# A pre-norm linear-attention and FFN block on one core: one more transpose by DMA, two more FFN blocks in halves, and a new order table

## The chip, the cores and the metric

The kernel runs on one core of a Trainium2 chip. The metric is the device time of one execution in microseconds. Before the change three timed executions took 169.82 (the median), 169.5 and 170.22 us. One further execution was profiled; it took 169.75 us by the same clock, and the span of its trace, from the first to the last instruction, is 168.0 us.

## The reference, cut to what matters

The input x has 2048 tokens of 512 elements; there are 32 heads of 16 elements, and the FFN is 1792 wide. All tensors are bf16.

```python
def _A_ref(x, wqkv, wo):                 # linear attention
    q, k, v = split(x @ wqkv)            # H = 32 heads of Dh = 16
    phi = lambda t: jnp.where(t > 0, t + 1, jnp.exp(t)) + 1e-6
    pq, pk = phi(q), phi(k)
    kv  = jnp.einsum("bhsd,bhse->bhde", pk, v)
    z   = jnp.einsum("bhsd->bhd", pk)
    num = jnp.einsum("bhqd,bhde->bhqe", pq, kv)
    den = jnp.einsum("bhqd,bhd->bhq", pq, z)[..., None] + 1e-6
    return concat_heads(num / den) @ wo
def _B_ref(x, w1, w2):                   # FFN
    return jnp.maximum(x @ w1, 0) @ w2
h  = x + _A_ref(_layernorm(x), wqkv, wo)
h2 = h + _B_ref(_layernorm(h), w1, w2)
```

## The kernel before

**Tiles and stages.** The 2048 tokens are 16 tiles of 128 (t = 0 to 15) in four chunks of 512 (c = 0 to 3). The first stage normalizes the tiles, transposes each (tokens move from partitions to columns, `lnT0` to `lnT3`, one for each chunk), and multiplies by the key and query weights. The keys go through phi and are multiplied with the normalized input into the four PSUM banks 4 to 7, which serve as one accumulator over all tiles; a sum over the keys gives z. The second stage turns the accumulator into `kv` and then into one matrix `m_sb` for each group of heads, divides the queries by the denominator (which goes through DRAM to be spread over the partitions, tile `rr`), and forms h. The third stage normalizes h, transposes it into the same `lnT` tiles, and runs the FFN: `w1` blocks of 128 columns (f = 0 to 13) for each chunk, and then for each tile two runs of seven products with `w2`.

**What sets the order.** Nothing is scheduled by a planner. The text `ORDER` lists every step, in the order in which it is written; each engine takes its own steps in the order of the list and waits by semaphores for what they need. A word is a step and its numbers:

- `lx`, `lk`, `lq`, `lv`, `lo`, `l1`, `l2`: loads of x and the weights, all on SP's DMA queue.
- `S`, `A`, `R`, `N` (`s`, `a`, `r`, `n`, `nA` for the second norm): statistics (VectorE, DVE for short), aggregate (DVE), 1/std (ScalarE, ACT), normalized tile (DVE; `nA` on ACT).
- `T.t.bank` with `E.t`: transpose of tile t on TensorE (PE), four products of 128 x 128 into a bank, and its copy to `lnT` on ACT. `X.t` (and `x.t` for the second norm): the same transpose by one DMA on SP's queue, without PE, PSUM and ACT.
- `K.t.bank`: four products of a tile with the key weights. `F`, `U` (ACT: exp, relu), `M`, `D` (DVE: min, sum) make phi of two tiles. `Q.c.j.bank` with `qF`, `qU`, `qM`, `qD`: the same for the queries.
- `G.t`: four products of tile t into the accumulator. `za`, `zf`, `zhi`, `zlo` (DVE), `z` (PE), `zc`, `zh` (DVE): the sum over the keys. `gA`, `gD`, `kv`, `kx`, `m`, `mA`, `mD`: from the accumulator to `m_sb`.
- `d4`, `dl4`, `dx4`, `wb`, `rb`, `ab`, `dm`: denominator, its reciprocal, its way through DRAM (`wb` writes, eight `rb` or `ab` read into `rr`), and the product with the queries. `h.t.bank` and `hD.t`: h of a tile, and its sum with x.
- `p.c.f.bank`: block f of chunk c for all 512 tokens, four products of 512 columns. `ph.c.f.bank.half`: the same for 256 tokens, four products of 256 columns into half of a bank. `pD` (DVE), `pA` (ACT): relu of two neighbouring blocks. `f.t.bank.f0.n`: n of the fourteen products of tile t with `w2`. `fo` (DVE), `fd` (SP): the output and its DMA.

The numbers also choose the PSUM bank, so a step waits for the last reader of its bank. PE takes about 900 products in the order of the list, and what stands behind a waiting product waits too. SP's queue holds the loads, the DMA transposes, the way of the denominator and the outputs, one behind the other.

The lines that the steps below rest on:

```python
op_X = lambda t: nc.sync.dma_start_transpose(out=lnT_of(t), in_=ln_nat[:, t, :])     # L314
op_x = lambda t: nc.sync.dma_start_transpose(out=lnT_of(t), in_=hn[:, t % NQ, :])    # L315
def op_ph(c, f, b, half):
    cols = slice(half * CW // 2, (half + 1) * CW // 2)
    for kd in range(KD):
        nc.tensor.matmul(bk[:, b, cols], lhsT=w1_sb[:, kd, f * P : (f + 1) * P],      # L526
                         rhs=lnT[c][:, kd, cols], ...)
for word in ORDER.split():
    name, *idx = word.split(".")
    ops[name](*map(int, idx))
```

Line numbers of the profile: L293 `T`, L303 `E`, L314 `X`, L322 `K`, L330 `Q`, L340/L343 `F`/`U` and their query forms, L347/L350 `M`/`D`, L374 `G`, L398 `z`, L477 `rb`, L493 `dm`, L502 `h`, L517 `p`, L526 `ph`, L537 `pD`, L546 `f`, L554 `fo`.

Of the kernel before, what the change touches and what calls it, by code (L numbers as in the profile page):

```python
# [16 lines left out]

ORDER = """
table const lx.0.1 warm.66.7.64 lx.1.1 masks lx.2.1 lk.0.4 lx.3.1 S.0 lx.4.2 S.1 lx.6.2 lq.0.4 A.0 A.1 S.2 R.0.1
warm.2.7 lx.8.4 R.1.1 N.0 lx.12.4 A.2 N.1 T.0.1 R.2.1 T.1.5 E.0 N.2 E.1 T.2.2 S.3 K.0.0 E.2 A.3 S.4 K.2.2.2.2  # L20
R.3.1 K.2.2.0.2 F.0.1 N.3 S.5 U.0.1 T.3.3 K.1.6.0.2 E.3 A.4 A.5 K.1.6.2.2 S.7 R.4.2 K.3.1.0.2 M.0.1 F.1.1 S.6
K.3.1.2.2 U.1.1 Q.0.1.5 N.4 F.2.1 A.6 N.5 A.7 F.3.1 T.4.6 M.1.1 X.5 D.0.1 Q.0.0.4 R.6.2 D.1.1 M.2.1 U.3.1 M.3.1
Q.0.2.0 N.7 lo.0.2 E.4 S.9 X.7 U.2.1 Q.0.3.1 N.6 qU.0.0.2 D.3.1 K.4.2 S.15 X.6 qF.0.0.2 S.8 K.5.3 D.2.1 qM.0.0.2
qF.0.2.2 G.3 A.8 A.9 S.12 R.8.2 G.0 S.14 F.4.2 N.9 G.2 A.12 N.8 X.9 U.4.2 S.13 G.1 A.15 A.14 A.13 qD.0.0.2 X.8
R.12.2 K.6.2 qU.0.2.2 M.4.2 S.11 K.7.3 lv.0.2 R.14.2 N.12 N.13 X.12 K.9.1 S.10 F.6.2 D.4.2 K.8.0 U.6.2 lv.2.2 A.10
M.6.2 X.13 G.4 N.14 U.8.2 N.15 D.6.2 G.5 X.15 F.8.2 za.4.1 G.6 A.11 X.14 M.8.2 K.12.0 R.10.2 qM.0.2.2 N.10 K.13.1
N.11 X.10 D.8.2 G.7 za.6.0 F.12.2 X.11 K.14.2 U.12.2 qD.0.2.2 K.15.3 M.12.2 l1.2.2 za.8.0 l2.0.7 K.10.0 F.14.2
D.12.2 K.11.1 U.14.2 zf G.9 M.14.2 F.10.2 D.14.2 G.8 U.10.2 zhi M.10.2 G.12 zlo D.10.2 G.14 z.1.0 z.2.0 z.3.0
z.0.0 G.15 zc zh d4.0.3 G.11 dl4.0 dx4.0 G.10 wb.0 G.13 lo.2.2 Q.1.0.1 gA.2.2 gD.0.2 rb.0.6 Q.1.1.2 ab.0.3 rb.0.2
ab.0.7 rb.0.4 kv.0.0 kv.2.0 ab.0.1 rb.0.0 kv.1.0 kv.3.0 ab.0.5 l1.0.2 Q.1.3.6 kx qF.1.0.2 Q.1.2.5 qU.1.0.2  # L30
qM.1.0.2 m.0.3 m.1.4 Q.2.3.7 qF.1.2.2 mD.0.2 Q.2.1.1 qU.1.2.2 qM.1.2.2 dm.0.0.2 m.2.3 m.3.4 Q.2.0.0 dm.0.2.2
mA.2.2 qD.1.0.2 h.1.6 qU.2.0.2 qD.1.2.2 h.0.2 hD.1 qF.2.0.2 h.3.3 s.1 hD.0 Q.2.2.6 a.1 s.0 nA.1 d4.1.2 a.0 h.2.1
hD.3 x.1 nA.0 s.3 qF.2.2.2 Q.3.0.5 x.0 a.3 hD.2 dl4.1 Q.3.3.4 n.3 qU.2.2.2 s.2 x.3 Q.3.2.3 a.2 dx4.1 n.2 Q.3.1.6
qM.2.0.2 qF.3.2.2 x.2 qM.2.2.2 ph.0.2.0.0 qU.3.2.2 qM.3.2.2 ph.0.3.1.0 wb.1 ph.0.0.2.0 qF.3.0.2 qD.3.2.2
ph.0.1.3.0 qD.2.2.2 ph.0.1.3.1 qU.3.0.2 ph.0.0.2.1 qM.3.0.2 rb.1.6 p.0.11.7 rb.1.3 pD.0.0.2 rb.1.1 ph.0.3.1.1
rb.1.0 p.0.10.6 qD.2.0.2 rb.1.7 qD.3.0.2 rb.1.4 p.0.9.2 rb.1.2 pD.0.10.2 rb.1.5 p.0.6.5 l2.7.7 d4.2.6.2 ph.0.2.0.1
dl4.2 p.0.5.4 r.0.4 dm.1.0.2 dl4.3 p.0.4.3 dx4.2 dm.1.2.2 h.4.7 pD.0.2.2 wb.2 pA.0.4.2 p.0.7.6 dx4.3 hD.4 p.0.8.1
pD.0.6.2 h.5.7 pD.0.8.2 rb.2.4 p.0.13.4 rb.2.7 rb.2.3 hD.5 h.6.5 rb.2.0 rb.2.6 f.1.2.0.7 hD.6 rb.2.5 s.5 rb.2.2
rb.2.1 p.0.12.3 wb.3 h.7.1 pD.0.12.2 f.0.7.7.7 hD.7 s.4 f.2.4.0.7 s.7 a.5 a.4 dm.2.0.2 f.1.2.7.7 n.4 dm.2.2.2 a.7
n.5 rb.3.2 s.6 rb.3.6 h.9.0 rb.3.3 h.8.1 x.4 hD.9 a.6 f.0.7.0.7 n.7 r.4.4 fo.1 x.7 n.6 s.9 f.3.5.0.7 rb.3.1 x.6  # L40
h.10.0 x.5 h.11.3 f.3.5.7.7 f.2.4.7.7 fo.3 hD.8 fd.3 rb.3.7 p.1.13.2 fo.2 rb.3.4 fd.1 hD.11 p.1.12.1 rb.3.5 a.9
fo.0 fd.2 p.1.2.6 rb.3.0 hD.10 p.1.3.7 pD.1.12.2 p.1.6.0 pD.1.2.2 p.1.0.3 dm.3.0.2 p.1.7.1 dm.3.2.2 h.13.7
pD.1.6.2 p.1.1.4 hD.13 p.1.4.5 pD.1.0.2 p.1.5.6 s.13 p.1.9.3 pD.1.4.2 h.12.7 p.1.8.2 hD.12 s.10 p.1.11.5 s.8
p.1.10.4 pD.1.8.2 h.14.1 s.11 h.15.7 hD.14 a.10 f.7.0.0.7 a.11 n.9 hD.15 n.11 pD.1.10.2 f.6.7.0.7 a.8 n.10 r.8.4
s.14 x.10 f.4.1.0.7 n.8 x.8 f.5.5.0.7 x.9 f.5.5.7.7 x.11 f.4.1.7.7 fo.5 fd.0 s.12 a.13 f.7.0.7.7 a.12 fo.4 a.14
f.6.7.7.7 fo.7 n.14 n.12 s.15 p.2.10.5 fo.6 p.2.11.6 n.13 fd.6 a.15 n.15 r.12.4 x.12 p.2.13.1 p.2.12.0 fd.5 x.13
p.2.9.4 pD.2.12.2 p.2.8.3 x.15 p.2.2.1 pD.2.8.2 x.14 p.2.3.2 pD.2.10.2 p.2.0.3 fd.7 pD.2.2.2 p.2.1.4 p.2.7.6
pD.2.0.2 p.2.6.5 p.3.8.1 pD.2.6.2 p.3.9.2 p.3.12.3 pD.3.8.2 p.3.13.4 p.3.2.0 pD.3.12.2 p.2.4.6 p.3.10.5 p.3.6.1
p.2.5.7 p.3.4.3 pD.2.4.2 p.3.5.4 p.3.7.2 f.11.7.0.7 pD.3.6.2 pD.3.4.2 f.11.7.7.7 p.3.3.1 f.10.3.7.7 pD.3.2.2
p.3.11.6 p.3.0.4 pD.3.10.2 f.8.1.0.7 f.10.3.0.7 p.3.1.5 f.8.1.7.7 pD.3.0.2 fo.10 f.15.0.0.14.3.1 f.15.6.0.14.0.2  # L50
fo.15.3.1 fd.15.3.1 f.13.4.0.7 fo.15.0.2 fd.15.0.2 fd.4 f.13.4.7.7 f.14.5.7.7 fo.13 fo.11 fd.13 fd.10 f.12.6.0.7
fo.8 fd.8 fd.11 f.14.5.0.7 f.9.7.0.7 f.9.7.7.7 f.12.6.7.7 fo.9 fo.14 fd.9 f.15.3.0.14.2.1 fd.14 fo.12 fd.12
fo.15.2.1 fd.15.2.1
"""

# [541 lines left out]
```

## Time and profile before

| quantity | value |
|---|---|
| timed executions | 169.5, 169.82 (median), 170.22 us |
| profiled execution | 169.75 us, span of its trace 168.0 us |
| PE busy | 161.2 us, 96% of the span |
| DVE busy | 114.3 us, 68% |
| ACT busy | 49.4 us, 29% |
| TensorE clock granted | 0.999 |
| DMA | 16.28 MB in 26091 packets |

A few matmul records are missing from the trace (896 matmuls beside 912 weight loads), so a single short hole between two products can be a missing record. PE is shown busy until the modelled end of a product; the products themselves follow each other at 0.216 us for 512 columns.

### The profile page before, as it was taken

The page shows a single profiled execution, that of the slowest core. Times are in us where ns is not written, and L with a number is a line of the kernel's source. Part 1 is how long each engine was busy: PE and PEld are TensorE (multiplying, and loading weights), DVE is VectorE, ACT ScalarE, POOL GpSimd, SP SyncE. Part 2 cuts the span into 40 slices and gives each one's busy share as a digit, 9 for nine tenths or more (in the row PEclk, how much of TensorE's full clock was granted, in tenths as well). Part 3 has the DMA queues.
Part 4 walks back from the last instruction along what each step waited for, and adds up shares of the span by engine and source line. Part 5 has one row for each costly group of instructions (what it writes and reads, how often), then busy time and mean ns, then how long its engine had stood idle before and what let it go on. Part 6 is the DMA issues. An engine that isn't in the chain of part 4 may idle for free.

```text
span 168.0 us, 2376 instructions
## 1 busy us (share of the span) xinstructions
PE 161.2 (96%) x896; PEld 78.3 (47%) x912; DVE 114.3 (68%) x215; ACT 49.4 (29%) x83; POOL 4.8 (3%) x21
## 2 busy tenths in 40 slices
...
GB/s 112 328 313 156 58 182 105 234 238 96 205 138 35 119 92 248 98 105 7 109 71 153 5 4 0 31 102 23 125 94 4 0 0 0 0 0 59 125 0 101
DMA packets 26091, 16.28 MB, mean 97 GB/s; under 512 B 16096, under 2 KB 25056, under 8 KB 26080
## 3 DMA queue, kind: packets, MB, share of 16 engines
...
q8 instruction: 7, 0.11, 0.3%
q14 instruction: 4, 0.03, 0.1%
HBM read 9.96 MB, written 2.62 MB: 75 GB/s over the span
## 4 chain that ended last, share of the span: by engine, by line
PE 84%; DVE 6%; DMA 4%; issue 1%; ACT 1%; SPq 1%; DVEq 0%
PE bk L546 29%; PE bk L517 27%; PE bk L374 8%; PE bk L322 7%; PE bk L502 6%; PE bk L330 4%; DMA x_nat<-in_A_x_dram 2%; DVE h_nat L508 2%; DMA lnT<-hn 1%; PE bk L526 1%; DVE st L256 1%; DVE st L254 1%; SPq L220 1%; DVE pqT L350 1%; PE bk L398 1%
## 5 line engine op out<-in xcount | busy, mean ns | idle before, releaser
L546 PE MATMUL bk<-w_sb,at 128*128 128x512 bf16 (+2 forms) x245 | 49.4, 355 | 0.4
L517 PE MATMUL bk<-lnT,w_sb 128*128 128x512 bf16 x205 | 46.7, 379 | 0.1
L537 DVE TENSOR_SCALAR at<-bk 128x1024 bf16<-128x1024 f32 x27 | 32.5, 1219 | 16.2 <-PE bk L517 15.0
L546 PEld LDWEIGHTS <-at 128*128 128x128 bf16 x252 | 23.5, 98 | 25.2 <-DVE at L537 0.3
L517 PEld LDWEIGHTS <-w_sb 128*128 128x128 bf16 x208 | 20.4, 98 | 23.9
L554 DVE SCALAR_TENSOR_TENSOR gT<-bk,rstd,h_nat 128x512 bf16<-128x512 f32 (+2 forms) x18 | 12.1, 685 | 19.3 <-PE bk L546 13.9
L260 ACT ACTIVATE rstd<-mv,eps 128x2 f32<-128x2 f32 (+2 forms) x14 | 4.1, 293 | 51.7 <-DVE mv L257 48.9
L340 ACT ACTIVATE eb<-bk 128x1024 bf16<-128x1024 f32 (+1 forms) x18 | 16.6, 931 | 4.4 <-PE bk L322 2.6
L343 ACT ACTIVATE rb<-bk 128x1024 bf16<-128x1024 f32 (+1 forms) x18 | 16.5, 930 | 0.0
L502 PE MATMUL bk<-m_sb,pqs 128*128 128x512 bf16 x64 | 15.6, 379 | 0.0
L330 PE MATMUL bk<-lnT,wq_sb 128*128 128x512 bf16 x61 | 15.0, 379 | 0.2
L322 PE MATMUL bk<-wk_sb,lnT 128*128 128x512 bf16 x64 | 14.8, 379 | 0.0
L374 PE MATMUL bk<-at,h_nat 128*128 128x512 bf16 x54 | 13.0, 379 | 0.1
L508 DVE TENSOR_TENSOR h_nat<-bk,x_nat 128x512 bf16<-128x512 f32 x16 | 10.9, 681 | 1.7 <-PE bk L502 1.7
L254 DVE BATCH_NORM_STATS2 st<-x_nat 128x6 f32<-128x512 bf16 x16 | 10.6, 677 | 2.0 <-DMA x_nat<-in_A_x_dram 2.0
L256 DVE BATCH_NORM_STATS2 st<-h_nat 128x6 f32<-128x512 bf16 x16 | 10.8, 685 | 0.1
L502 PEld LDWEIGHTS <-pqs 128*128 128x128 bf16 x64 | 6.2, 98 | 7.6 <-DVE pqs L493 0.5
L374 PEld LDWEIGHTS <-h_nat 128*128 128x128 bf16 x64 | 6.1, 98 | 7.3 <-issue 0.2
L330 PEld LDWEIGHTS <-wq_sb 128*128 128x128 bf16 x64 | 6.2, 98 | 7.1
L322 PEld LDWEIGHTS <-lnT 128*128 128x128 bf16 x64 | 5.9, 98 | 7.5 <-DMA lnT<-h_nat 0.7
L347 DVE TENSOR_SCALAR eb<-eb 128x1024 bf16<-128x1024 bf16 (+1 forms) x18 | 6.7, 386 | 0.7 <-ACT eb L340 0.7
L493 DVE TENSOR_TENSOR pqs<-pqT,rr 128x1024 bf16<-128x1024 bf16 x8 | 5.2, 680 | 1.9 <-DMA rr<-scr 1.9
...
## 6 DMA issues: line engine op xcount, KB each, us to landing
w_sb<-in_B_w_dram SPq DMA_DIRECT2D x4, 896.0 KB, 5.0
...
```

Of the source, the lines that this page charges most:

```text
L254: op_S = lambda t: nc.vector.bn_stats(out=st[:, t, :], in_=x_nat[:, t, :])
L256: op_s = lambda t: nc.vector.bn_stats(out=st2[:, t, :], in_=h_nat[:, t, :])
L322: nc.tensor.matmul(bk[:, b, :], lhsT=lnT[c][:, kd, j * P : (j + 1) * P], rhs=wk_sb[:, kd, :], **part(("k", t), KD),)
L330: nc.tensor.matmul(bk[:, b, :], lhsT=wq_sb[:, kd, j * P : (j + 1) * P], rhs=lnT[c][:, kd, :], start=(kd == 0), stop=(kd == KD - 1),)
L340: nc.scalar.activation(out=buf(eb, kind, i, n), in_=bank(at_bank[kind, i], n), func=ACT.Exp)
L343: nc.scalar.activation(out=buf(rb, kind, i, n), in_=bank(at_bank[kind, i], n), func=ACT.Relu)
L374: nc.tensor.matmul(bk[:, KD + kd, :], lhsT=ln_nat[:, t, kd * P : (kd + 1) * P], rhs=pk(t)[:, 0, :], start=(not stated), stop=(len(stated) ...
L502: nc.tensor.matmul(bk[:, b, :], lhsT=pqs[:, (c * KD + jb) % NQ, j * P : (j + 1) * P], rhs=m_sb[:, jb, :], start=(jb == 0), stop=(jb == KD ...
L508: nc.vector.tensor_tensor(out=h_nat[:, t : t + n, :], in0=bank(at_bank["h", t], n), in1=x_nat[:, t : t + n, :], op=ALU.add,)
L517: nc.tensor.matmul(bk[:, b, :], lhsT=w1_sb[:, kd, f * P : (f + 1) * P], rhs=lnT[c][:, kd, :], start=(kd == 0), stop=(kd == KD - 1),)
L537: nc.vector.tensor_scalar(out=acts[c % 2][:, f : f + n, :], in0=bank(at_bank["p", c, f], n), scalar1=-1.0, scalar2=0.0, op0=ALU.mult, op1= ...
L546: nc.tensor.matmul(bk[:, b, 0 : w * P], lhsT=acts[c % 2][:, f, j * P : (j + 1) * P], rhs=w2_sb[:, f, k * P : (k + w) * P], **part(("f", t, ...
```

## The change

Only the text `ORDER` is changed; no step's code is.

- Tile 4 of the first norm: `T.4.6` and `E.4` are gone, `X.4` is there instead.
- The first chunk's FFN blocks 10 and 11 are now written in halves, as 0 to 3 were: six blocks of half 0 stand ahead of the first block of half 1, where it was four.
- The order of nearly all other steps and the banks of most are new.

A few lines of the diff; all that is changed reads like this:

```diff
-K.3.1.2.2 U.1.1 Q.0.1.5 N.4 F.2.1 A.6 N.5 A.7 F.3.1 T.4.6 M.1.1 X.5 D.0.1 Q.0.0.4 R.6.2 D.1.1 M.2.1 U.3.1 M.3.1
+N.5 Q.0.3.1 M.0.1 X.5 F.1.1 A.7 A.6 D.0.1 R.6.2 Q.0.0.6 N.4 M.1.1 U.3.1 N.6 X.4 Q.0.1.7 N.7 U.2.1 D.1.1 F.2.1 S.8
...
-qM.2.0.2 qF.3.2.2 x.2 qM.2.2.2 ph.0.2.0.0 qU.3.2.2 qM.3.2.2 ph.0.3.1.0 wb.1 ph.0.0.2.0 qF.3.0.2 qD.3.2.2
-ph.0.1.3.0 qD.2.2.2 ph.0.1.3.1 qU.3.0.2 ph.0.0.2.1 qM.3.0.2 rb.1.6 p.0.11.7 rb.1.3 pD.0.0.2 rb.1.1 ph.0.3.1.1
+n.2 qD.2.0.2 x.2 ph.0.2.6.0 qF.3.2.2 qM.2.2.2 ph.0.0.2.0 qD.2.2.2 ph.0.3.7.0 qF.3.0.2 rb.1.5 qM.3.2.2 ph.0.1.3.0
+rb.1.3 ph.0.11.1.0 qU.3.0.2 rb.1.1 qM.3.0.2 ph.0.10.0.0 qD.3.2.2 rb.1.6 ph.0.10.0.1 rb.1.7 qD.3.0.2 ph.0.3.7.1
```

**SP's queue, first norm.** The rows from the last loads of x to the first load of an FFN weight, before; `lnT1` to `lnT3` take the tiles of chunks 1 to 3, and one row can stand for several DMAs (x2, x3).

```order
L220 DMA x_nat_70<-in_A_x_dram 128x2048 x2
L314 DMA_TRANSPOSE lnT1_86<-h_nat_84 128x4x128
L226 DMA wo_sb_74<-in_A_wo_dram 128x2x512
L314 DMA_TRANSPOSE lnT1_86<-h_nat_84 128x4x128 x2
L314 DMA_TRANSPOSE lnT2_87<-h_nat_84 128x4x128 x2
L226 DMA wv_sb_73<-in_A_wqkv_dram 128x2x512
L314 DMA_TRANSPOSE lnT3_88<-h_nat_84 128x4x128
L226 DMA wv_sb_73<-in_A_wqkv_dram 128x2x512
L314 DMA_TRANSPOSE lnT3_88<-h_nat_84 128x4x128 x3
L314 DMA_TRANSPOSE lnT2_87<-h_nat_84 128x4x128 x2
L226 DMA w1_sb_75<-in_B_w1_dram 128x2x1792
```

The same place now:

```order
L220 DMA x_nat_70<-in_A_x_dram 128x2048 x2
L314 DMA_TRANSPOSE lnT1_86<-h_nat_84 128x4x128 x4
L226 DMA wv_sb_73<-in_A_wqkv_dram 128x2x512 x2
L314 DMA_TRANSPOSE lnT2_87<-h_nat_84 128x4x128 x2
L314 DMA_TRANSPOSE lnT3_88<-h_nat_84 128x4x128 x4
L314 DMA_TRANSPOSE lnT2_87<-h_nat_84 128x4x128 x2
L226 DMA w1_sb_75<-in_B_w1_dram 128x2x1792
```

Chunk 1 has four DMA transposes instead of three, the load of `wo` is out of their way, and both loads of the value weights stand ahead of the eight transposes of chunks 2 and 3, which are now unbroken.

**SP's queue, second norm of chunk 0.** From the way of the first denominators (`scr0`, `rr`) to that of the third (`scr2`), before and then now; the four transposes into `lnT0` are `x.1`, `x.0`, `x.3`, `x.2` in both.

```order
L477 DMA rr_113<-scr0_114 16x4x512 x4
L226 DMA w1_sb_75<-in_B_w1_dram 128x2x1792
L315 DMA_TRANSPOSE lnT0_85<-hn_119 128x4x128 x4
L474 DMA scr1_115<-rd_112 128x512
L477 DMA rr_113<-scr1_115 16x4x512 x8
L226 DMA w2_sb_76<-in_B_w2_dram 128x7x512
L474 DMA scr2_116<-rd_112 128x512
L477 DMA rr_113<-scr2_116 16x4x512 x8
```

```order
L477 DMA rr_113<-scr0_114 16x4x512 x4
L226 DMA w2_sb_76<-in_B_w2_dram 128x7x512
L315 DMA_TRANSPOSE lnT0_85<-hn_119 128x4x128 x2
L474 DMA scr1_115<-rd_112 128x512
L315 DMA_TRANSPOSE lnT0_85<-hn_119 128x4x128 x2
L477 DMA rr_113<-scr1_115 16x4x512 x8
L474 DMA scr2_116<-rd_112 128x512
L226 DMA w2_sb_76<-in_B_w2_dram 128x7x512
L474 DMA scr3_117<-rd_112 128x512
L477 DMA rr_113<-scr2_116 16x4x512 x8
```

The write of the second denominators (`wb.1`, into `scr1`) has moved between the second and the third transpose; the first half of `w2` (`l2.0.7`), which was loaded in the first stage, is now loaded between `wb.2` and `wb.3`, ahead of the eight reads of `scr2`.

**DVE, second norm of chunk 0.** From `hD.3` (sum with x of tile 3) on, before and then now; L276 is the normalized tile that a DMA transpose waits for, `n.3` first, `n.2` second.

```order
L508 TENSOR_TENSOR h_nat_84<-bk_120,x_nat_70 128x512
L256 BN_STATS st2_106<-h_nat_84 128x6
L257 BN_AGGR mv2_107<-st2_106 128x2
L508 TENSOR_TENSOR h_nat_84<-bk_120,x_nat_70 128x512
L276 TENSOR_SCALAR hn_119<-h_nat_84,mv2_107 128x512
L256 BN_STATS st2_106<-h_nat_84 128x6
L257 BN_AGGR mv2_107<-st2_106 128x2
L276 TENSOR_SCALAR hn_119<-h_nat_84,mv2_107 128x512
```

```order
L508 TENSOR_TENSOR h_nat_84<-bk_120,x_nat_70 128x512
L256 BN_STATS st2_106<-h_nat_84 128x6
L508 TENSOR_TENSOR h_nat_84<-bk_120,x_nat_70 128x512
L257 BN_AGGR mv2_107<-st2_106 128x2
L347 TENSOR_SCALAR eb_109<-eb_109 128x1024
L276 TENSOR_SCALAR hn_119<-h_nat_84,mv2_107 128x512
L256 BN_STATS st2_106<-h_nat_84 128x6
L257 BN_AGGR mv2_107<-st2_106 128x2
L276 TENSOR_SCALAR hn_119<-h_nat_84,mv2_107 128x512
```

One min of the queries (L347, `qM.2.0`) has moved ahead of `n.3`.

More of the change, by code (lines that the diff above doesn't have):

```diff
@@ L19 @@
 table const lx.0.1 warm.66.7.64 lx.1.1 masks lx.2.1 lk.0.4 lx.3.1 S.0 lx.4.2 S.1 lx.6.2 lq.0.4 A.0 A.1 S.2 R.0.1
-warm.2.7 lx.8.4 R.1.1 N.0 lx.12.4 A.2 N.1 T.0.1 R.2.1 T.1.5 E.0 N.2 E.1 T.2.2 S.3 K.0.0 E.2 A.3 S.4 K.2.2.2.2
-R.3.1 K.2.2.0.2 F.0.1 N.3 S.5 U.0.1 T.3.3 K.1.6.0.2 E.3 A.4 A.5 K.1.6.2.2 S.7 R.4.2 K.3.1.0.2 M.0.1 F.1.1 S.6
-K.3.1.2.2 U.1.1 Q.0.1.5 N.4 F.2.1 A.6 N.5 A.7 F.3.1 T.4.6 M.1.1 X.5 D.0.1 Q.0.0.4 R.6.2 D.1.1 M.2.1 U.3.1 M.3.1
-Q.0.2.0 N.7 lo.0.2 E.4 S.9 X.7 U.2.1 Q.0.3.1 N.6 qU.0.0.2 D.3.1 K.4.2 S.15 X.6 qF.0.0.2 S.8 K.5.3 D.2.1 qM.0.0.2
@@ L24 @@
[L24 to L33, printed above, removed]
@@ L34 @@
-qM.2.0.2 qF.3.2.2 x.2 qM.2.2.2 ph.0.2.0.0 qU.3.2.2 qM.3.2.2 ph.0.3.1.0 wb.1 ph.0.0.2.0 qF.3.0.2 qD.3.2.2
-ph.0.1.3.0 qD.2.2.2 ph.0.1.3.1 qU.3.0.2 ph.0.0.2.1 qM.3.0.2 rb.1.6 p.0.11.7 rb.1.3 pD.0.0.2 rb.1.1 ph.0.3.1.1
-rb.1.0 p.0.10.6 qD.2.0.2 rb.1.7 qD.3.0.2 rb.1.4 p.0.9.2 rb.1.2 pD.0.10.2 rb.1.5 p.0.6.5 l2.7.7 d4.2.6.2 ph.0.2.0.1
-dl4.2 p.0.5.4 r.0.4 dm.1.0.2 dl4.3 p.0.4.3 dx4.2 dm.1.2.2 h.4.7 pD.0.2.2 wb.2 pA.0.4.2 p.0.7.6 dx4.3 hD.4 p.0.8.1
-pD.0.6.2 h.5.7 pD.0.8.2 rb.2.4 p.0.13.4 rb.2.7 rb.2.3 hD.5 h.6.5 rb.2.0 rb.2.6 f.1.2.0.7 hD.6 rb.2.5 s.5 rb.2.2
@@ L39 @@
[L39 to L52, printed above, removed]
+warm.2.7 lx.8.4 R.1.1 lx.12.4 A.2 N.0 R.2.1 N.1 T.0.6 N.2 T.1.4 E.0 T.2.1 E.1 K.0.6 S.3 A.3 S.5 K.1.7.0.2 R.3.1
```

29 lines of the change are left out of this document (added).

## The prediction, made before the changed kernel was run

> **What bounds the kernel now.** First the page: busy shares and the shares of the chain that ended last.
>
> ```profile
> span 168.0 us, 2376 instructions
> PE 161.2 (96%) x896; PEld 78.3 (47%) x912; DVE 114.3 (68%) x215; ACT 49.4 (29%) x83; POOL 4.8 (3%) x21
> PE 84%; DVE 6%; DMA 4%; issue 1%; ACT 1%; SPq 1%; DVEq 0%
> ```
>
> PE is the bound, and both reorderings can only win what PE loses in waits. So the second view is the busy time by stage, with the cuts set where the chain leaves PE (columns: window, then PE, PEld, DVE, ACT, POOL busy with counts, clock, DMA share, GB/s).
>
> ```profile
> 6.70:36.30 29.60, 29.42 (x178) 13.72 (x179) 27.87 (x69) 23.79 (x42) 0.00 (x0) 1.00 0.69 199
> 36.30:56.10 19.80, 19.62 (x106) 8.98 (x108) 13.67 (x27) 13.90 (x17) 0.00 (x0) 1.00 0.39 108
> 56.10:58.70 2.60, 2.00 (x18) 1.63 (x18) 1.75 (x5) 2.60 (x4) 0.00 (x0) 1.00 0.58 124
> 58.70:165.00 106.30, 105.52 (x522) 49.99 (x531) 67.17 (x102) 5.71 (x14) 0.00 (x0) 1.00 0.21 59
> ```
>
> From 6.7 us on PE is full but for the third window: 0.60 us idle in 2.6. What remains in the fourth row is mostly missing records and the end of PE's work before 165. The third view, PE's timeline and the chain there, says what the hole is (start, duration, then the group).
>
> ```profile
> 56.09 1.92 PE L526 MATMUL bk<-lnT,w_sb 128*128 128x256 bf16 x16
> 58.62 1.03 PE L526 MATMUL bk<-lnT,w_sb 128*128 128x256 bf16 x8 [0.60 <-DMA lnT<-hn]
> ...
> 56.14 2.43 DMA lnT<-hn
> 59.65 0.86 PE bk L517 x4
> 60.51 0.44 PE bk L526 x4
> ```
>
> The sixteen products of the four half-0 blocks start at 56.09. A block in halves costs 0.44 for four products, 0.109 each, against 0.86 in full, so they are through at 56.09 + 16 x 0.109 = 57.84. The next product, of half 1, needs `x.2`, issued at 56.14 and landed 2.43 later, at 58.57. It starts at 58.62: **0.78 us lost**, of which the profile calls 0.60 idle because it lets the last product end 0.17 after its issue slot.
>
> **The change part by part.** The sum is made against the profiled execution, 169.75 us, which lies 0.07 under the median, 169.82.
>
> *Six blocks in halves.* Work: two more blocks cost 2 x (2 x 0.44 - 0.86) = 0.04 at most. Cover: six half-0 blocks fill 6 x 0.44 = 2.62 us, two blocks or 0.87 more than now. The hole goes if `x.2` lands no more than 0.1 later relative to PE. The rows behind `x.2`:
>
> ```profile
> 49.63 0.69 DVE L256 BATCH_NORM_STATS2 st<-h_nat 128x6 f32<-128x512 bf16 x1
> 50.83 0.17 DVE L257 BATCH_NORM_AGGREGATE mv<-st 128x2 f32<-128x6 f32 x1
> 51.78 5.57 SPq L315 DMA_TRANSPOSE lnT<-hn  x4
> 57.45 0.53 SPq L474 DMA_DIRECT2D scr<-rd  x1
> 51.04 1.58 ACT L282 ACTIVATE hn<-h_nat,mv 128x512 bf16<-128x512 bf16 x2 [1.00 <-DVE mv L257]
> 53.90 0.35 DVE L276 TENSOR_SCALAR hn<-h_nat,mv 128x512 bf16<-128x512 bf16 x1
> 55.09 0.35 DVE L276 TENSOR_SCALAR hn<-h_nat,mv 128x512 bf16<-128x512 bf16 x1
> ```
>
> Now SP's queue binds itself: `n.3` is done at 54.25 and `n.2` at 55.44, and SP comes to `x.2` at 56.14, 4.36 after `x.1`, and to `x.3` one transpose (1.3) earlier. In the new order `a.1` no longer stands behind `hD.0`: it can start when `s.1` ends, at 50.36 instead of 50.83, so `nA.1` (51.04) and `x.1` (51.78) come 0.48 earlier, `x.1` at 51.30. `wb.1` (0.53, and 0.05 to the next) goes ahead of `x.3`. `x.2` is then issued at 51.30 + 4.36 + 0.58 = 56.24, 0.1 later than now. The min ahead of `n.3` and the later `a.3` push `n.3` and `n.2` by 0.43, to 54.68 and 55.87; both still come ahead of SP, by 0.2 and 0.4. `x.2` lands at 56.24 + 2.43 = 58.67, half 1 starts at 58.72, and PE has filled until 58.7. So 0.87 more work is done and half 1 starts 0.1 later: **-0.77**. (The 0.05 that the first half-0 product now waits for `x.0` lies inside this stretch.)
>
> Who pays: `wb.1` is issued at 54.3, 3.1 us earlier than now, which feeds `rb.1` sooner; `h.6` needs it only at 66. Banks: each half-0 block's bank was last read by an `hD` or by phi of the queries; the latest is `qF.3.2`, which by my count of ACT's steps ends at 57.3, ahead of block 11 at 57.8.
>
> *T.4 to X.4.* PE loses four products of 128 x 128, ACT the copy `E.4`, SP gets one more transpose.
>
> ```profile
> 11.69 0.22 PE bk L293 x4
> 12.91 0.59 ACT L303 ACTIVATE lnT<-bk 128x512 bf16<-128x512 bf16 x1
> 13.57 6.91 SPq L314 DMA_TRANSPOSE lnT<-h_nat  x4
> 23.12 6.44 SPq L314 DMA_TRANSPOSE lnT<-h_nat  x5
> DMA to landing us min/median/max: 2.4/2.4/3.1
> ```
>
> Five transposes in a row take 6.44 us of the queue, 1.29 each; one lands 2.4 after its issue, 3.1 behind a weight load. `X.4` stands behind `X.5`, where SP waits (the four from 13.57 on take 6.91, where four without waits take 5.2), so it costs the queue nothing later. By my count of DVE's steps `X.5` is issued at 11.0 and `X.4` at 12.4; it lands at 14.8, and `K.4` comes at 14.98 by PE's sum. PE gains **-0.22** if the end of this stage follows PE. That is not sure, since DVE is nearly full here too (27.87 of 29.60):
>
> ```profile
> 31.97 1.03 ACT L340 ACTIVATE eb<-bk 128x1024 bf16<-128x1024 f32 x1
> 34.07 0.68 DVE L350 TENSOR_TENSOR at<-rb,eb 128x1024 bf16<-128x1024 bf16 x1
> 31.70 3.62 PE L374 MATMUL bk<-at,h_nat 128*128 128x512 bf16 x16
> 35.15 0.19 PE L398 MATMUL bk<-ones,zhl 128*128 128x1 bf16 x2
> ```
>
> PE starts `z` at 35.15 with DVE's last sum (`D.10`) done at 34.75: DVE is 0.4 ahead. In the new order `D.10` is last again, DVE has the same steps, and I count one wait of 0.24 (`M.10` for `F.10`, which follows `K.11`, done at 31.4), so about 34.85, while PE comes to `z` at 34.87 and to the columns of `D.10` 0.1 later. Bounds: -0.22 if PE sets it, 0 if DVE does; I take **-0.22**, to which PE's row is nearer.
>
> *Order of the first stage.* The keys' products wait for transposes twice now; one shows in two rows of PE's timeline; the third row is `N.9`, and the row of the list of waits has both as seen by the weight load (total, times, longest).
>
> ```profile
> 27.29 1.03 PE L374 MATMUL bk<-at,h_nat 128*128 128x512 bf16 x4
> 28.21 1.04 PE L322 MATMUL bk<-wk_sb,lnT 128*128 128x512 bf16 x4
> 17.56 0.40 DVE L268 TENSOR_SCALAR h_nat<-x_nat,mv,rstd 128x512 bf16<-128x512 bf16 x1
> PEld L322 <- DMA lnT<-h_nat: 0.7, 2, 0.4
> ```
>
> 27.29 + 4 x 0.216 = 28.15, and `K.14` starts at 28.21: 0.05, with the second 0.07 in all. The weight loads `lv` no longer split the transposes, so these go: **-0.07**. In their place come near misses. `N.9` moves behind one more statistic, to about 18.05 (17.56 now), and `X.9` goes out as it ends. Then `X.9` lands at 20.9 and the others follow at 1.29: `X.12` 23.5, `X.15` 26.1, `X.10` 28.7. PE's sum brings `K.9` at 21.03, `K.12` at 23.62, `K.15` at 26.21, `K.10` at 28.80. Each has 0.1 in hand, and each is the same lateness, not a new one. Bounds: 0 if my count of DVE's steps is exact, +0.6 if the transposes land at 3.1 instead of 2.4; I take **+0.2**, nearer to 0 because the loads that make 3.1 are out of the way.
>
> *Rest of the order.* From 59 us on PE has the same products. I followed its banks and `lnT` tiles through the new list; the tightest places are `p.1.3` (bank 5 free just as it comes, 0 to 0.1) and the first block of chunk 2's `lnT` and of chunk 1's, with 0.5 in hand. The end is the same piece, the last 128 columns of tile 15. **0**, with +0.1 as the upper bound.
>
> Sum: 169.75 - 0.77 + 0.04 - 0.22 - 0.07 + 0.2 = 168.9 us.
>
> *A rule against it.* The rows put 0.22 for four products on PE beside 2.4 from issue to landing of one DMA. The Trainium skill, VectorE: DVE Perf Modes, sections "The three transpose paths" and "Rules for kernel authors", gives 390 ns for TensorE and 1309 ns for the DMA on 128 x 128, and advises TensorE where PSUM will do as the destination. Worked with its figures alone, as an estimate, a tile would come 1309 - 390 = 0.9 us later, and with no cover the sum would be 168.9 + 0.2 + 0.9 = 170.0. The trace agrees on which of the two is slower, with a wider gap; its durations are used here.
>
> **The rivals.** *The added transpose is on the path.* (This is the case that the rule of the skill speaks for.) `X.4` or the row behind it lands late: at 3.1 instead of 2.4, `K.4` waits 0.5, or `K.9` 0.6, and the later ones keep that pace. For it: 3.1 has been seen, and the margins are 0.1. Against: in the trace 3.1 occurs only behind a weight load. 168.9 - 0.2 + 0.6 = 169.3.
>
> *The hole stays in part.* `x.2` is late by more than the fill: 0.4 later if `wb.1`, waiting for ACT, holds `x.3`, or `n.2` is late. Then 168.9 + 0.4 = 169.3.
>
> *Slower: the half of `w2` that now comes late.*
>
> ```profile
> 63.01 0.43 SPq L226 DMA_DIRECT2D w_sb<-in_B_w_dram  x1
> 66.15 0.34 SPq L474 DMA_DIRECT2D scr<-rd  x1
> 68.56 3.88 SPq L477 DMA_DIRECT2D rr<-scr  x8
> w_sb<-in_B_w_dram SPq DMA_DIRECT2D x4, 896.0 KB, 5.0
> 71.53 1.08 PE bk L546 x5
> ```
>
> `l2.0.7`, 896 KB, now goes out behind `wb.2`, at about 63.7, and takes 5 us: landed at 69. The first product with it, now at 71.5 and 1.7 of other work later less what is won, comes at about 72. `rb.2` stands behind it, and two of its eight issues wait for its landing; `dm.2`, `rb.3`, `dm.3`, `n.5` and the next four transposes hang on them, with block 1 of chunk 1 at 91 at the end, which decides at about the same point. So up to 72 it costs nothing, then a microsecond for each; landing at 74, after 10.3 us, with eight reads of `rr` in its way, makes 168.9 + 2 = 170.9. Against: 3 us in hand.
>
> **How the numbers follow.** A measurement can tell about 0.5% from no change: 0.85 us, so below 168.97 is faster and above 170.67 slower. Forecast as summed, 0.58: it lies 0.07 from the line, and its own unknowns (0 to 0.6, 0 to 0.22, 0 to 0.1) go to both sides; most of it (0.45) below, 0.13 within. The transpose on the path 0.17 and the hole in part 0.10: within 0.5% but for 0.05 together. Late `w2` 0.10, slower. Something unnamed in a list laid out anew 0.05: 0.03 slower, 0.02 within. Faster 0.50, same 0.37, slower 0.13. The range: down to 168.4, the sum without the +0.2 and with 0.3 for places where I counted DVE too slow; up to 170.0, the 0.4 of the hole, the 0.6 of the transpose in place of 0.2, 0 for the -0.22, and the 0.1 of the rest at once; the late `w2` is left out.
>
> **What would show it.** In the trace after: PE's idle before L526 on `lnT<-hn` falls from 0.60 to under 0.15, with 24 products of half 0 in a row; four products of L293 fewer; `z` (L398) starts at 34.9 against 35.15. Wrong would be: waits of PEld L322 for `lnT<-h_nat` above 0.7 together, `z` at 35.2 or later, a wait of L546 for `in_B_w_dram` near 72, or of L517 for `lnT<-hn` near 91.

## The result, and the profile after

The changed kernel takes **169.34 us** (median, 168.88 to 170.18 in 20 runs) beside 170.23 us for the kernel before on the same chip (169.5 to 172.34, 20 runs): a ratio of **0.9953, 95% interval 0.9938 to 0.9969**. The ratio leaves out an execution that is more than 1.5% above the fastest of its kernel (here 172.34); the quotient of the two medians is 0.9948. Its profiled execution took 169.0 us against 169.75 before; 168.9 was forecast.

The page of the kernel after, busy shares and chain:

```profile
span 167.3 us, 2392 instructions
PE 162.4 (97%) x916; PEld 79.3 (47%) x916; DVE 114.5 (68%) x215; ACT 48.9 (29%) x82; POOL 4.7 (3%) x21
PE 89%; DMA 4%; ACT 2%; DVE 2%; SPq 1%; issue 0%
```

PE's share of the chain went from 84% to 89%. The busy time by stage says where (columns as before; the cuts follow the chain of the kernel after, up to 0.2 us from those of before):

```profile
6.70:36.30 29.60, 29.50 (x175) 13.54 (x174) 27.79 (x69) 23.56 (x42) 0.00 (x0) 1.00 0.69 201
36.30:55.90 19.60, 19.60 (x110) 8.99 (x107) 13.57 (x27) 13.70 (x17) 0.00 (x0) 1.00 0.41 118
55.90:58.60 2.70, 2.70 (x25) 2.33 (x24) 2.23 (x5) 2.70 (x4) 0.00 (x0) 1.00 0.50 99
```

The third window had 0.60 us of idle PE and now has none. PE's timeline there, with SP's queue:

```profile
51.37 2.72 SPq L315 DMA_TRANSPOSE lnT<-hn  x2
54.18 0.53 SPq L474 DMA_DIRECT2D scr<-rd  x1
54.81 2.50 SPq L315 DMA_TRANSPOSE lnT<-hn  x2
...
56.09 4.97 PE L526 MATMUL bk<-lnT,w_sb 128*128 128x256 bf16 x44
60.99 0.40 PE L446 MATMUL bk<-pqT,zhd 128*32 128x512 bf16 x4
```

All halved products but those of one half (44 of 48) run in one row without a break, 24 of them half 0. The hole is gone, as the prediction had it.

The first stage is the other place. The start shifts from one profile to the next: `T.3`, which waits for the normalized tile 3, began anywhere between 8.63 and 9.62 us in the twelve profiles of this study. So the stage is read from `T.3` (L293) to `z` (L398). The timeline after:

```profile
8.66 0.40 PE L293 MATMUL bk<-ident,h_nat 128*128 128x128 bf16 x4
...
10.93 5.61 SPq L314 DMA_TRANSPOSE lnT<-h_nat  x4
...
15.19 0.55 PEld L322 LDWEIGHTS <-lnT 128*128 128x128 bf16 x4 [0.59 <-DMA lnT<-h_nat]
...
18.33 10.36 SPq L314 DMA_TRANSPOSE lnT<-h_nat  x8
...
21.37 0.55 PEld L322 LDWEIGHTS <-lnT 128*128 128x128 bf16 x4 [0.45 <-DMA lnT<-h_nat]
...
35.19 0.19 PE L398 MATMUL bk<-ones,zhl 128*128 128x1 bf16 x2
```

The SPq rows are the four transposes of chunk 1 and the eight of chunks 2 and 3; the PEld rows are the weight loads of `K.4` and `K.9`. The chain has `X.4` itself, from issue to landing, and the list of waits has the sum of such waits:

```profile
12.68 2.47 DMA lnT<-h_nat
```

```profile
PEld L322 <- DMA lnT<-h_nat: 1.2, 3, 0.6
```

And `T.3` in the timeline of before:

```profile
8.71 0.40 PE L293 MATMUL bk<-ident,h_nat 128*128 128x128 bf16 x4
```

Before, 35.15 - 8.71 = 26.44 us from `T.3` to `z`; after, 35.19 - 8.66 = 26.53, with four products fewer. `K.4` waits for `X.4`, and `K.9` for `X.9`: the products themselves start 0.26 and 0.12 later than without a wait. From `z` to the end of the execution it is 169.75 - 35.15 = 134.60 before and 169.0 - 35.19 = 133.81 after, -0.79. The three parts, -0.05 (start), +0.09 (first stage) and -0.79, make the -0.75. **In these two profiles the whole gain lies behind `z`.**

### The profile page after: what moved, and what is told of

Read it like the earlier page. It is cut to its first block, busy times and chain, and to the rows that moved or that the text cites. A ratio compares the mean times of both kernels' runs of the same rounds, so it can differ in the third digit from the quotient of the medians.

```text
span 167.3 us, 2392 instructions
## 1 busy us (share of the span) xinstructions
PE 162.4 (97%) x916; PEld 79.3 (47%) x916; DVE 114.5 (68%) x215; ACT 48.9 (29%) x82; POOL 4.7 (3%) x21
## 4 chain that ended last, share of the span: by engine, by line
PE 89%; DMA 4%; ACT 2%; DVE 2%; SPq 1%; issue 0%
PE bk L546 28%; PE bk L517 26%; PE bk L374 8%; PE bk L502 8%; PE bk L330 6%; PE bk L322 6%; PE bk L526 3%; DMA x_nat<-in_A_x_dram 2%; DMA lnT<-h_nat 1%; SPq L220 1%; PE bk L446 1%; DVE gT L554 1%; ACT lnT L303 1%; PE bk L398 1%; ACT rb L343 1%; ACT eb L340 1%
## 5 line engine op out<-in xcount | busy, mean ns | idle before, releaser
L546 PE MATMUL bk<-w_sb,at 128*128 128x512 bf16 (+2 forms) x252 | 49.9, 355 | 0.0
L517 PE MATMUL bk<-lnT,w_sb 128*128 128x512 bf16 x200 | 44.5, 379 | 0.0
L537 DVE TENSOR_SCALAR at<-bk 128x1024 bf16<-128x1024 f32 x27 | 32.0, 1220 | 17.6 <-PE bk L517 17.3
L517 PEld LDWEIGHTS <-w_sb 128*128 128x128 bf16 x200 | 19.6, 98 | 23.4
L322 PE MATMUL bk<-wk_sb,lnT 128*128 128x512 bf16 x64 | 15.5, 379 | 0.1
L502 PE MATMUL bk<-m_sb,pqs 128*128 128x512 bf16 x64 | 15.0, 379 | 0.0
L322 PEld LDWEIGHTS <-lnT 128*128 128x128 bf16 x64 | 5.9, 98 | 7.9 <-DMA lnT<-h_nat 1.2
L347 DVE TENSOR_SCALAR eb<-eb 128x1024 bf16<-128x1024 bf16 (+1 forms) x18 | 6.9, 387 | 1.4 <-ACT eb L340 1.4
L268 DVE TENSOR_SCALAR h_nat<-x_nat,mv,rstd 128x512 bf16<-128x512 bf16 x16 | 6.1, 409 | 0.0
```

The lines of the kernel that those rows point to most:

```text
L322: nc.tensor.matmul(bk[:, b, :], lhsT=lnT[c][:, kd, j * P : (j + 1) * P], rhs=wk_sb[:, kd, :], **part(("k", t), KD),)
L502: nc.tensor.matmul(bk[:, b, :], lhsT=pqs[:, (c * KD + jb) % NQ, j * P : (j + 1) * P], rhs=m_sb[:, jb, :], start=(jb == 0), stop=(jb == KD ...
L517: nc.tensor.matmul(bk[:, b, :], lhsT=w1_sb[:, kd, f * P : (f + 1) * P], rhs=lnT[c][:, kd, :], start=(kd == 0), stop=(kd == KD - 1),)
L537: nc.vector.tensor_scalar(out=acts[c % 2][:, f : f + n, :], in0=bank(at_bank["p", c, f], n), scalar1=-1.0, scalar2=0.0, op0=ALU.mult, op1= ...
L546: nc.tensor.matmul(bk[:, b, 0 : w * P], lhsT=acts[c % 2][:, f, j * P : (j + 1) * P], rhs=w2_sb[:, f, k * P : (k + w) * P], **part(("f", t, ...
```

## The experiments

The theory was that the filled hole is the gain; the rival, that it is the first stage. The first four runs do one part alone, or undo one.

**Two blocks back to full, in the changed kernel** (its banks and order kept).

```diff
-ph.0.11.1.0 qU.3.0.2 rb.1.1 qM.3.0.2 ph.0.10.0.0 qD.3.2.2 rb.1.6 ph.0.10.0.1 ... ph.0.11.1.1
+qU.3.0.2 rb.1.1 qM.3.0.2 qD.3.2.2 rb.1.6 p.0.10.0 ... p.0.11.1
```

> The changed kernel with four half-0 blocks instead of six: blocks 10 and 11 in full, behind the wait for x.2, all else as changed. Theory (the hole filled): the wait comes back with 0.8 us, and the time is that of the kernel before, ratio 0.999 to 1.001. Rival (the gain is the first stage and the rest of the order): ratio 0.9955 to 0.997.

0.9997 (0.9978 to 1.0017): the gain is gone. PE's timeline has the hole again, 16 products in halves and then a wait for `x.2`:

```profile
56.10 1.91 PE L526 MATMUL bk<-lnT,w_sb 128*128 128x256 bf16 x16
58.70 1.02 PE L517 MATMUL bk<-lnT,w_sb 128*128 128x512 bf16 x4 [0.69 <-DMA lnT<-hn]
```

Against the changed kernel the two halved blocks are worth 0.9997 - 0.9953 = 0.0044, or 0.75 us, give or take 0.4, since the two ratios come from different sets of executions.

**Tile 4 by DMA alone, in the kernel before.**

```diff
-... F.3.1 T.4.6 M.1.1 X.5 ... E.4
+... F.3.1 M.1.1 X.4 X.5 ...
```

> The kernel before with the other named part alone: T.4 and E.4 gone, X.4 directly ahead of X.5 on SP's queue. Theory (the hole filled): PE is rid of 0.22 us, X.5 is issued 1.3 to 1.7 us later and K.5 waits for it by 0.2 to 0.4 us, so the start of z moves by 0 to +0.2 us and the time by the same, ratio 1.000 to 1.001. Rival (the gain is the first stage): z starts 0.2 us earlier or more and the ratio is 0.9985 or lower.

1.0005 (0.9988 to 1.0021): nothing, as expected. Two views of it: in PE's timeline the products of `K.5` (in this order `K.4` comes first) start 0.49 later than without a wait, since `X.5` now stands behind `X.4`, and the list of waits has more for the weight loads (total, times, longest; 0.7, 2, 0.4 before):

```profile
15.39 1.04 PE L322 MATMUL bk<-wk_sb,lnT 128*128 128x512 bf16 x4 [0.33 <-DMA lnT<-h_nat]
```

```profile
PEld L322 <- DMA lnT<-h_nat: 1.3, 3, 0.8
```

**One block more in halves, in the kernel before.**

```diff
-ph.0.1.3.0 qD.2.2.2 ... p.0.11.7
+ph.0.1.3.0 ph.0.11.7.0 qD.2.2.2 ... ph.0.11.7.1
```

> The kernel before with block 11 alone in halves: five half-0 blocks ahead. Theory (the hole filled): one block fills 0.436 us, so the wait for x.2 falls from 0.78 to 0.34 and the time by 0.43 us, ratio 0.9975. Rival (the gain is the first stage): ratio 0.999 to 1.001.

0.9978 (0.9964 to 0.9992), a hit by the time: half of the gain. Its own profile shows less. The wait for `x.2` falls to 0.34 between products, but `d4.2`, whose banks DVE's `pD.0.10` has to read first, now waits 0.35 where it was 0.1:

```profile
63.29 0.62 PE L446 MATMUL bk<-pqT,zhd 128*32 128x512 bf16 x8 [0.19 <-DVE at L537]
```

From `T.3` (8.69 here) it takes 169.62 - 8.69 = 160.93 us, only 0.11 less than before (169.75 - 8.71 = 161.04). So half of the hole is filled, and part of what that wins is already taken back behind it.

**Both blocks in halves, in the kernel before.** The same with `ph.0.10.6.0` and `ph.0.10.6.1`.

> The kernel before with one part of the change alone: FFN blocks 10 and 11 of chunk 0 in halves, the two half-0 blocks ahead of the first half-1 block, all else in the old order. Theory (the hole filled): PE's wait for x.2 near 58 us, 0.78 us, goes to zero, and the time falls by 0.75 us, ratio to before 0.9955; this is all of the change's gain. Rival (the gain is the first stage: no transpose of tile 4 on PE, new order): the hole goes too but the 0.8 us come back as waits before 66 us, ratio 0.999 to 1.001.

1.0013 (0.9996 to 1.0031): **missed.** The hole is filled, but what it held comes back as waits. PE's timeline and, below it, the busy time by stage:

```profile
56.96 4.30 PE L526 MATMUL bk<-lnT,w_sb 128*128 128x256 bf16 x37
...
64.36 0.61 PE L446 MATMUL bk<-pqT,zhd 128*32 128x512 bf16 x8 [0.45 <-DVE at L537]
```

```profile
62.50:72.00 9.50, 9.05 (x49) 4.09 (x49) 7.76 (x10) 3.71 (x7) 0.00 (x0) 1.00 0.58 171
```

The first product of `d4.2` goes into banks 6 and 7, where blocks 10 and 11 lay, and waits for DVE's `pD.0.10` to read them: 0.61 us between products, where it was 0.1. Another 0.17 is lost at block 9, which waits for its bank. This run's `T.3` began at 9.62, so its profiled time, 170.65, is compared from there: 161.03 against 169.75 - 8.71 = 161.04 before. So -0.73 for the hole, +0.51 and +0.17 for the two waits, and some hundredths: nothing left. The rival had said that the 0.8 us would come back as waits before 66 us, and they did; its reason, the first stage, is not what this shows, since from `T.3` to `z` this kernel takes 26.45 us and before 26.44.

**The same, with block 5 moved in front of these two waits.**

```diff
-p.0.9.2 ... p.0.6.5 l2.7.7 d4.2.6.2 ph.0.2.0.1 dl4.2 p.0.5.4
+p.0.5.4 p.0.9.2 ... p.0.6.5 l2.7.7 d4.2.6.2 ph.0.2.0.1 dl4.2
```

> The kernel before with six half-0 blocks (11 and 10 added), and full block 5 of chunk 0 moved ahead of block 9, so ahead of the second pair of d4 (banks 6 and 7). Theory (the hole is filled, and in the version without this move the gain went into waits for DVE behind it: 0.17 us at block 9 and 0.61 us at d4 for banks 6 and 7): 0.86 us of work now stands in front of both, they fall under 0.1 us together, and the whole is -0.77 + 0.04 + 0 to 0.2, a ratio of 0.9955 to 0.997. Rival (halves alone gain nothing, what they fill is taken back by the reads of rr or by DVE's sums wherever PE comes next): 0.999 to 1.001, with a wait of 0.4 us or more at another place between 62 and 74 us.

0.9995 (0.9982 to 1.0008): **missed again.** Both waits are gone, and the next step is late instead (timeline, then busy time by stage):

```profile
52.00 6.02 SPq L315 DMA_TRANSPOSE lnT<-hn  x4
...
56.76 4.42 PE L526 MATMUL bk<-lnT,w_sb 128*128 128x256 bf16 x39 [0.33 <-DMA lnT<-hn]
...
65.83 1.29 DVE L493 TENSOR_TENSOR pqs<-pqT,rr 128x1024 bf16<-128x1024 bf16 x2 [1.82 <-DMA rr<-scr]
66.58 1.21 PE L502 MATMUL bk<-m_sb,pqs 128*128 128x512 bf16 x4 [0.31 <-DVE pqs L493]
```

```profile
62.50:72.00 9.50, 9.19 (x50) 3.78 (x49) 7.40 (x9) 3.60 (x7) 0.00 (x0) 1.00 0.51 170
```

`h.4` waits for `dm.1`, which waits for the reads `rb.1`: 0.47 and 0.16 between products. In this profile the four transposes also held the queue for 6.02 us, where it was 5.57, and the first halved product waited 0.5 for `x.0`. By the time and by the wait of 0.47 this is what the rival had forecast; the next run decides against it.

**And with these waits cleared too.** DVE idled 1.8 us ahead of `dm.1`, so a sum that is ready goes there, and `h.4` and `h.5` go behind blocks that are ready.

```diff
-dm.1.0.2 ... h.4.7 pD.0.2.2 ... p.0.7.6 dx4.3 hD.4 p.0.8.1 pD.0.6.2 h.5.7 ... p.0.13.4 ... h.6.5
+pD.0.2.2 dm.1.0.2 ... p.0.7.6 dx4.3 p.0.8.1 pD.0.6.2 h.4.7 hD.4 ... p.0.13.4 h.5.5 ... h.6.7
```

> The kernel before with six half-0 blocks, block 5 ahead of block 9, and what stood in the way behind it moved too: the sum pD.0.2 ahead of dm.1 on VectorE (which idled 1.8 us there for the reads of rr), h.4 behind blocks 7 and 8, h.5 behind block 13. Theory (the filled hole is worth 0.73 us, but TensorE then comes sooner to work that in the order before was only just ready: d4 for its banks, h.4 for rr and for the bank that dl4.3 frees; the gain stays only where that work is moved back): no wait over 0.15 us between 58 and 72 us but the two of 0.1 us beside d4, and a ratio of 0.9955 to 0.9975. Rival (in the order before something else, VectorE's or the reads' own pace, takes the gain back wherever the waits are put): 0.999 to 1.001, with 0.5 us or more of waits in that stretch.

**0.9961 (0.9947 to 0.9975)**, a hit: the gain is there. PE's timeline and the busy time by stage have no idle left in either stretch behind the hole:

```profile
56.62 4.64 PE L526 MATMUL bk<-lnT,w_sb 128*128 128x256 bf16 x41
```

```profile
58.70:62.50 3.80, 3.80 (x32) 2.92 (x30) 2.99 (x5) 1.08 (x2) 0.00 (x0) 1.00 0.30 92
62.50:72.00 9.50, 9.50 (x52) 4.22 (x51) 7.92 (x11) 3.61 (x7) 0.00 (x0) 1.00 0.57 169
```

From `T.3` (9.17 here) it takes 169.52 - 9.17 = 160.35 us, against 161.04 before and 169.0 - 8.66 = 160.34 for the changed kernel. This version has tile 4 on TensorE and the old first stage.

**Is it the earlier `wb.1`?** In the changed order the reads `rb.1` go out sooner. Undone:

```diff
-qM.2.0.2 wb.1 qF.2.2.2 ... qD.2.0.2 x.2
+qM.2.0.2 qF.2.2.2 ... qD.2.0.2 x.2 wb.1
```

> The changed kernel with wb.1 behind x.2 in SyncE's queue, as before, so that the reads rb.1 go out some 1 us later. Theory (what lets the gain through is the order of TensorE's work, with h.6 as the first user of rr behind blocks 13 and 12): dm.1 is done at about 65.7 instead of 64.95 and h.6 comes at 66.1, so it costs nothing, while x.2 lands 0.6 us earlier: ratio to the kernel before 0.9945 to 0.996. Rival (the earlier wb.1 is what lets the gain through): a wait of 0.5 us or more at h.6 or at dm.2, ratio 0.998 or more.

0.9955 (0.9941 to 0.9968): it costs nothing. `x.2` was forecast to land 0.6 us earlier and did not: it went out at 56.16, and at 56.09 in the changed kernel. `dm.1` starts at 65.44, later than the 64.4 of the estimate, and `h.6`, the first product that needs it, follows at 66.47 without a wait:

```profile
65.44 1.29 DVE L493 TENSOR_TENSOR pqs<-pqT,rr 128x1024 bf16<-128x1024 bf16 x2 [1.56 <-DMA scr<-rd]
...
66.47 1.89 PE L502 MATMUL bk<-m_sb,pqs 128*128 128x512 bf16 x8
```

So the earlier reads are not needed. With the run before, what is left to let the gain through is the order of PE's work and its banks: `d4.2` in banks 4 and 5, and blocks 7, 4, 5, 13 and 12 between it and the first `h`. Which of these moves are needed was not tried one by one.

**Tile 4 back on TensorE, in the changed kernel.**

```diff
-X.4 Q.0.1.7 ... F.3.1
+Q.0.1.7 T.4.5 ... F.3.1 E.4
```

> The changed kernel with tile 4 transposed by TensorE again (T.4 behind Q.0.1, its copy E.4 on ScalarE, no X.4), all else as changed. Theory (the 0.22 us that X.4 takes off TensorE comes back as K.4's wait of 0.26 us): TensorE gets four products of 0.054 us more and K.4 waits no longer; z within 0.1 us of its place, ratio to the kernel before 0.9945 to 0.996. Rival (X.4 is worth its 0.22 us): z 0.2 us later, ratio 0.9965 to 0.9975.

0.994 (0.9924 to 0.9956), a little below the range that was forecast, outside that of the rival, and not to be told from the changed kernel. No weight load waits for a DMA transpose now. `T.3` and `z` in PE's timeline, and SP's queue from the `lv` loads on:

```profile
9.09 0.40 PE L293 MATMUL bk<-ident,h_nat 128*128 128x128 bf16 x4 [0.43 <-DVE h_nat L268]
...
35.44 0.19 PE L398 MATMUL bk<-ones,zhl 128*128 128x1 bf16 x2
...
15.77 1.27 SPq L226 DMA_DIRECT2D wv_sb<-in_A_wqkv_dram  x2
18.77 10.35 SPq L314 DMA_TRANSPOSE lnT<-h_nat  x8
```

`z` is 0.25 later than in the changed kernel, but `T.3` is 0.43 later: it takes 26.35 us from `T.3` to `z`, with 0.22 more work than the 26.53 of the changed kernel. Both waits are gone, 0.26 at `K.4` and 0.12 at `K.9`. The second goes as well because the row of chunk 1 is one transpose shorter: the queue is done with the `lv` loads 1.7 us ahead of `X.9` and not 0.7 (16.59 + 1.08 to 18.33 in the changed kernel), and `X.9` lands 2.4 after its issue, where it took 3.0. So the DMA transpose gave back what it saved.

**What made the transposes late.** `N.5` ahead of `S.6`, so that `X.5` and `X.4` go out sooner, and the loads `lv` behind `lo.2.2`, out of the way of `X.9`.

```diff
-R.4.2 K.3.3.0.2 S.6 ... N.5 Q.0.3.1 ... lv.2.2 ... lv.0.2 ... lo.2.2
+R.4.2 N.5 K.3.3.0.2 S.6 ... Q.0.3.1 ... lo.2.2 lv.2.2 lv.0.2
```

> The changed kernel with N.5 one place earlier on VectorE (ahead of S.6) and with the two weight loads lv behind lo in SP's queue, out of the way of X.9. Theory (what the first stage lost are the waits of K.4 for X.4, 0.26 us, and of K.9 for X.9, 0.12 us): both fall under 0.1 us together, z starts 0.3 us earlier, the ratio to the kernel before goes from 0.9953 to 0.993 to 0.994. Rival (VectorE's last sum sets the end of that stage, or the load moved behind comes late): z where it is, ratio 0.995 to 0.997.

0.9952 (0.9936 to 0.9968): the time missed, the waits in part. `K.4` waits no longer, `K.9` 0.05, and `X.9` lands 2.4 after its issue. PE's timeline, `T.3` and `z`, and the row of the list of waits:

```profile
8.86 0.40 PE L293 MATMUL bk<-ident,h_nat 128*128 128x128 bf16 x4
...
35.16 0.19 PE L398 MATMUL bk<-ones,zhl 128*128 128x1 bf16 x2
```

```profile
PEld L322 <- DMA lnT<-h_nat: 1.4, 4, 0.4
```

26.30 us, 0.23 less than the changed kernel's profile, and still four weight loads that wait a little: PE now comes sooner to transposes that leave the queue at their own pace. But the 0.23 is within what the changed first stage shows from one execution to the next. Of the kernels that leave this stage as the change has it, the one with two blocks back to full has 26.34 us from `T.3` to `z`, the one with `wb.1` moved 26.61, and the last one, with `w2` moved, 26.24. The timelines of these three, in that order:

```profile
8.86 0.40 PE L293 MATMUL bk<-ident,h_nat 128*128 128x128 bf16 x4 [0.21 <-DVE h_nat L268]
...
35.20 0.19 PE L398 MATMUL bk<-ones,zhl 128*128 128x1 bf16 x2
```

```profile
8.76 0.40 PE L293 MATMUL bk<-ident,h_nat 128*128 128x128 bf16 x4
...
35.37 0.19 PE L398 MATMUL bk<-ones,zhl 128*128 128x1 bf16 x2
```

```profile
8.85 0.40 PE L293 MATMUL bk<-ident,h_nat 128*128 128x128 bf16 x4 [0.20 <-DVE h_nat L268]
...
35.09 0.19 PE L398 MATMUL bk<-ones,zhl 128*128 128x1 bf16 x2
```

The first stage of before does not vary like this: the five profiles that have it show 26.44 to 26.46. What varies is two waits, and they account for all of it (us; waits between products):

| kernel | `X.5` holds the queue | `K.4` waits | `X.9`, issue to landing | `K.9` waits | `T.3` to `z` |
|---|---|---|---|---|---|
| changed | 1.65 | 0.26 | 3.0 | 0.12 | 26.53 |
| two blocks back to full | 1.32 | 0 | 2.8 | 0.19 | 26.34 |
| `wb.1` moved | 1.55 | 0.18 | 3.1 | 0.28 | 26.61 |
| `w2` moved | 1.29 | 0 | 2.7 | 0.09 | 26.24 |

Take the 0.22 of the four products and the 0.07 of the old waits off 26.44, add the two waits of a row, and its last column comes out to 0.01.

**The late half of `w2`, made later.**

```diff
-dx4.3 l2.0.7 dm.1.2.2 ... rb.2.3
+dx4.3 dm.1.2.2 ... rb.2.3 l2.0.7
```

> The changed kernel with the load of the late half of w2 (l2.0.7, 896 KB) behind the last of the rb.2 reads in SP's queue. Theory of the slower rival (the first product with it comes at 72 us, and from there each microsecond of lateness costs one): issued at about 69, it lands at about 74.3 after 5 us, so TensorE waits about 2.2 us before L546: ratio to the kernel before 1.006 to 1.011. Rival (there is other slack, or the reads of rr come sooner without it and pay part back): a wait under 1 us and a ratio below 1.002.

1.0052 (1.0034 to 1.007), 1.7 us above the changed kernel, a little under the forecast. The timeline of SP's queue and of PE:

```profile
68.94 0.42 SPq L226 DMA_DIRECT2D w_sb<-in_B_w_dram  x1
...
74.12 2.12 PE L546 MATMUL bk<-w_sb,at 128*128 128x512 bf16 x9 [1.72 <-DMA w_sb<-in_B_w_dram]
```

The load goes out at 68.94 and PE starts 5.18 later; the wait is 1.88 between products, and from `z` to the end it takes 170.79 - 35.09 = 135.70, which is 1.89 longer than the 133.81 of the changed kernel. Beyond 72 us the lateness of this load counts one for one here, as the rival had it. In the changed kernel it goes out at 63.64; being 5.30 later costs 1.88, so there it has 3.4 us in hand.

## Why the prediction was right, and where not

- **The hole (-0.77 + 0.04): right, in mechanism and size.** `x.1` went out at 51.37 (51.30 worked out), `x.2` at 56.09 (56.24), half 1 started without a wait. Behind `z` the profile gained 0.79, and undoing the two halves loses 0.75. It repeats: the five profiles with the hole filled and nothing waiting behind it (the changed kernel, the last version of the kernel before, and those with `wb.1`, tile 4 or `N.5` moved) take 133.79 to 133.89 us from `z` to the end, where before takes 134.60. What the runs add is that "from 59 us on PE has the same products" is not enough for the zero of the rest. In the order before the same six halves were worth nothing, since `d4.2` and then `h.4` came before their banks and reads were ready. The prediction had followed the banks of the new list, and there the zero holds; that the gain depends on it, it does not say.
- **Tile 4 (-0.22): the work went, and what it set off took the time back.** Two steps failed. `X.4` behind `X.5` was to land at 14.8, 0.2 ahead of `K.4`. `X.5` went out at 10.93, as worked out, but held the queue for 1.65, so `X.4` went out 1.75 later, where 1.4 was worked out (1.29 is the pace of a row of five), and it landed at 15.15: `K.4` waited 0.26. In two of the four profiles with this first stage it was 1.4, and `K.4` did not wait. The other step is "so it costs the queue nothing later". With one transpose more in chunk 1's row the `lv` loads are issued just ahead of `X.9`, which then lands 2.7 to 3.1 after its issue, and `K.9` waits in all four; with tile 4 on TensorE it lands in 2.4, and `K.9` does not wait.
- **The near misses (+0.2): right in kind, a little small.** "The loads that make 3.1 are out of the way" was wrong for `X.9`, as just told: `K.9`'s weight load comes 21.37 - 18.33 = 3.04 after its issue. In the changed kernel's profile the other three came in time. `K.4` and `K.9` together wait 0.09 to 0.46, in the mean 0.28. So the first stage was forecast at -0.22 - 0.07 + 0.2 = -0.09 and measured +0.09 in the changed kernel's profile; over the four profiles that share it (26.53, 26.34, 26.61, 26.24) the mean is 26.43, and before has 26.44: nothing gained. The waits of L322 came to 1.2, a sign that the prediction had named for the rival *the added transpose is on the path*, and `z` at 35.19 is at the edge of the other, 35.2. That rival was half true: it has the two right places, but they wait up to 0.28 each, not 0.5 or 0.6. DVE's bound did not show: PE's work and these two waits make up the whole stage.
- **The rule of the Trainium skill** (VectorE: DVE Perf Modes, "The three transpose paths"), that a DMA transpose takes longer than TensorE's: the trace agrees, for tiles four times as wide, with 2.47 from issue to landing of `X.4` beside 0.22 of PE and a copy of 0.59. That the DMA still costs nothing here is cover, and it is just used up: 26.35 with TensorE, 26.24 to 26.61 with the DMA.
- **The rivals.** The hole in part did not come: `wb.1` did not hold up `x.3`. The late `w2` did not come either, and its point of 72 us was right.
- **The number.** 168.9 was forecast against 169.0 for the profiled run and 169.34 for the median. The median of before was 170.23 in the same runs, where the forecast stood on 169.82: as a ratio 0.9946 was forecast and 0.9953 measured. The prediction's line for faster, 0.5%, lies inside the interval, so its 0.50 for faster against 0.37 for the same is not decided. That the sum comes so near is in part luck: the forecast was 0.08 too low for the first stage, by the mean, and 0.06 too high for the part behind `z`.
